# Attention means on chip, one load for the values, and the first weight loads among the keys and queries

## The chip, the cores and the metric

One core of one Trainium2 chip runs one program. The metric is the device time of that program in microseconds. The engines named below are PE (matrix products), DVE (VectorE), ACT (ScalarE), POOL (GpSimd) and SP, which here only issues DMAs.

## The reference

Inputs are q, k and v of 4 batches, 8 heads, 768 tokens and 64 features, and the parameters of a gated two-layer network. Every block of 32 tokens has a summary: the maximum of its keys and the mean of its values. Each query attends to the tokens less than 16 away and to the 24 summaries. The result goes through the network, token by token.

```python
k_sum = k.reshape(B, H, nb, block, D).max(axis=3)
v_sum = v.reshape(B, H, nb, block, D).mean(axis=3)
scores_l = np.where(|i - j| < 16, scale * q @ k.T, -1e9)
scores_s = scale * q @ k_sum.T + log(block)
a = softmax(concat(scores_l, scores_s))
x = a @ concat(v, v_sum)                  # (4, 768, 512) after joining heads
xk, xr = mix(mu_k, x, x_prev), mix(mu_r, x, x_prev)
out = sigmoid(xr @ w_r) * (relu(xk @ w_k)**2 @ w_v)
```

The network's weights come in 64-bit words, which the kernel turns into floats on chip.

## The kernel before, in words

**Attention.** Heads are taken in pairs: four pairs a batch, each a *set* with two *units* (the halves of the tokens, six windows of 64 queries each). A window sees 120 rows: 64 tokens, 24 summaries, 32 tokens. `load_set` (L302) loads the keys `kt` and, per half, the values `vx`: rows 0 to 63 by one DMA (L312), rows 88 to 119 by another (L315). DVE reduces the keys (L325 to L337). The mean of the values goes into rows 64 to 87. In batch 0 that is done from `vx` itself: POOL clears rows 64 to 87 (L346), PE multiplies each of the 12 windows by a shifted 120 x 24 pooling matrix and adds all 12 up in one PSUM tile (L350), ACT copies the sum out (`vm`, L367), and one DMA per half spreads it over the six windows (L370). The other batches take the means from a load of transposed values (L361 to L365) and spread them by the same DMAs. `unit` (L375) is then: scores on PE (L396), mask and row minimum on DVE (L407), exponential on ACT (L411), reciprocal on DVE (L417, L418), normalisation on POOL (six instructions a unit, L423), transposes on PE (L430), their copy on ACT (L434), products with the values on PE (L443), copy to `vx` (L454 on DVE or L456 on ACT).

**Network.** Work goes in eight half batches n. `mixes` makes the shifted blends, split in a high and a low part (L466 to L477); `gate_tile` is 12 matmuls of 512 columns against `wr` (L489 to L491) and a sigmoid (L495); `experts` goes over eight slices j, with 12 matmuls against `wk` (L510), relu, square and split (L515 to L521), 9 matmuls against `wv` (L531). The gates of n = 1 are put between the slices j = 1, 2, 3 of n = 0.

**Weights.** `weight` (L252) handles one of 20 pieces (4 `wr`, 8 `wk`, 8 `wv`) of 512 KB: a load into one of three `st` buffers (L260); a scaling on ACT (L268) or POOL (L271); three bit operations on DVE (L275, L278, L282); a cast on ACT (L290); a difference on DVE (L292).

**Order.** Nothing is issued in the order written. Each operation has a length from the table `LENGTH`, sometimes a second engine it may run on, and a due time. `Plan.schedule` (L111) hands due times back from users to producers (less the length and `SLACK`) and then simulates the five engines; at each step it places the operation that can start first, the most urgent where several can, and where there are two engines takes the one that would finish first. A load may be placed no sooner than 15 us (`EARLY`) before it is due, and its simulated rate is `DMA_NS_PER_BYTE`. The order of each engine that comes out is fixed: a real engine waits for its next instruction even if a later one is ready. The `wr` pieces have no due time of their own (L579), only that handed back from the gates.

```python
start, need, ok = max(at, now, o.due - EARLY if e == "SP" else 0), {}, True
...
if any(max(start, engines[f]) + c < start + o.ways[e][0] for f, (c, _) in o.ways.items() if f != e):
    continue
```

Of the kernel before, what the change touches and what calls it, by code (L numbers as in the profile page):

```python
# [29 lines left out]
HW = NW // 2  # L30
# [8 lines left out]
LENGTH = dict(  # L39
    score=900, transpose=340, vtrans=200, vpool=2800, values=1000, gate=2790, gate32=3720, e1=2090, e1_32=2800,  # L40
    e2a=1400, e2b=700, e2=700, e2_32=2800, e2l_32=930,
    kred=860, kred2=470, kmax=190, kcopy=340, vred=860, mask=204, rc=310, evac=475, mixd=535, sub=475, khv=300,
    result=695, wbits=340, wor=612, wsub=612, tiny=60,
    exp=380, pts=380, vm=160, mixa=520, cast=405, relu=525, square=435, sigmoid=500, wscale=570, wcast=530,
    norm=455, wscale_p=900, mixa_p=750, kcopy_p=600, evac_a=480, fill=900,
)
TAIL = dict(PE=0, DVE=85, ACT=95, POOL=0, SP=0)
LATENCY = dict(PE=260, DVE=110, ACT=110, POOL=150, SP=0)
DMA_NS_PER_BYTE = 1 / 290.0
DMA_FIXED = 2000  # L50
# [23 lines left out]
class Plan:  # L74
# [36 lines left out]
    def schedule(self):  # L111
# [83 lines left out]
@with_exitstack  # L195
def tile_kernel(ctx: ExitStack, tc: tile.TileContext, q, k, vT, v, mask, ident, pool, mu, w_k, w_v, w_r, out):
    nc = tc.nc
# [3 lines left out]
    def tiles(name, n, shape, dtype=F32, pool=const):  # L201
        return [pool.tile(shape, dtype, name=f"{name}{i}") for i in range(n)]
# [48 lines left out]

    def weight(name, i, src, dst_h, dst_l):  # L252
        st, we, wc = buf("st"), buf("we"), buf("wc")
# [31 lines left out]
        op("SP", "load", None, load, writes=[(st, 0)], size=P * 4096)  # L285
        op("ACT", "wscale", None, scale_act, reads=[(st, 0)], writes=whole, other=("POOL", "wscale_p", scale_pool))
# [12 lines left out]
    def windows(vw):  # L299
        return vw.t[0:NK, 0:S].rearrange("p (w d) -> p w d", d=P)  # L300

    def load_set(b, p):  # L302
# [39 lines left out]
        if b == 0:  # L342
            tp = buf("mm")

            for x in vw:
                op("POOL", "fill", None, lambda x=x: nc.gpsimd.memset(x.t[QW:KB, 0:S], 0.0), writes=[(x, "b")])  # L346
# [7 lines left out]
            op("PE", "vpool", None, means, reads=[(x, y) for x in vw for y in "abc"] + [*POOLM], writes=[(tp, 0)])  # L354
# [12 lines left out]
        op("ACT", "vm", None, lambda: nc.scalar.activation(  # L367
            vm.t, tp.t[0:NS, 0:P], AF.Copy, scale=1.0 / BLOCK if b else 1.0), reads=[(tp, 0)], writes=[(vm, 0)])
        for x in vw:
            op("SP", "load", None, lambda x=x: nc.sync.dma_start(  # L370
                out=windows(x)[QW:KB], in_=vm.t.unsqueeze(1).broadcast_to([NS, HW, P])),
               reads=[(vm, 0)], writes=[(x, "b")], size=NS * HW * 512)
        return e

    def unit(b, p, hf, e, due):  # L375
# [62 lines left out]
        def values():  # L438
# [252 lines left out]
```

## Time and profile before

| | |
|---|---|
| runs | 480.15 us median of 3 (479.31 to 1084.43) |
| the profiled execution's own time | 480.32 us |
| its span, first to last instruction | 478.5 us |
| mean granted PE clock | 0.966 |
| PE busy | 450.2 us (94%) |
| DVE, ACT, POOL busy | 275.4, 290.9, 125.4 us |

The profile covers one execution. A busy time is that of an engine over a stretch; idle time ahead of an instruction is put down to what ended it. L-numbers are lines of the kernel before.

### The profile page before, as it was taken

Reading aid. Unit: us, or ns where it says so; the run is one execution under the profiler, and the core shown is the slowest. Engines: PE = TensorE matmul, PEld = TensorE weight load, DVE = VectorE, ACT = ScalarE, POOL = GpSimd, SP = SyncE. Lnnn points to the kernel's source line nnn. Section 1 sums busy time; section 2 is a strip of 40 time slices with the busy share of each in tenths; the row PEclk is TensorE's granted clock in tenths of the full one; section 3 lists DMA queues with packets and bytes.
Section 4 is the critical chain, followed back from the end, with each engine's and each line's share of the span. In section 5 each row is a group of like instructions: output and inputs, shape, how many; then the busy total and the mean of one; then the engine's idle time right before and its main releaser. Section 6 shows DMA issues by size and latency. Waiting matters only on the chain.

```text
span 478.5 us, 9637 instructions
## 1 busy us (share of the span) xinstructions
PE 450.2 (94%) x3468; PEld 378.4 (79%) x3468; DVE 275.4 (58%) x876; ACT 290.9 (61%) x810; POOL 125.4 (26%) x258
## 2 busy tenths in 40 slices
PE   4878797889999999999999999999999999999996
PEld 3656585769888888888788888997788888888995
DVE  2669997779955486527454566429355564222223
ACT  3659789796778656527895565528886555231321
POOL 5527903205135402301433302202242302000000
PEclk9987589799999999999999999999999999999999
DMA  8896328775510119605200309806100010001001
GB/s 262 193 270 176 115 85 270 215 236 172 172 53 14 42 44 301 165 0 184 77 14 14 110 2 284 189 0 209 28 10 8 14 47 20 0 1 66 1 0 66
DMA packets 27893, 49.38 MB, mean 103 GB/s; under 512 B 3399, under 2 KB 16455, under 8 KB 27847
## 3 DMA queue, kind: packets, MB, share of 16 engines
q1 hardware_dynamic: 27847, 48.79, 35.2%
q8 instruction: 27, 0.44, 0.4%
q14 instruction: 19, 0.16, 0.1%
HBM read 40.12 MB, written 6.29 MB: 97 GB/s over the span
## 4 chain that ended last, share of the span: by engine, by line
PE 77%; ACT 6%; DVE 2%; issue 1%; POOL 1%; POOLq 0%; ACTq 0%
PE mm L531 27%; PE mm L510 26%; PE mm L489 4%; PE av L443 4%; PE mm L490 4%; PE mm L491 4%; PE pt L430 4%; PE sc L396 3%; ACT y L411 2%; ACT L411 1%; POOL y L423 1%; ACT L495 1%; ACT wc L268 1%; DVE wc L282 0%; ACT wv_h L290 0%
## 5 line engine op out<-in xcount | busy, mean ns | idle before, releaser
L423 POOL TENSOR_SCALAR y<-y,rc 128x120 f32<-128x120 f32 x192 | 87.2, 472 | 173.2 <-DVE rc L418 154.7
L510 PE MATMUL mm<-xs,wk_h 128*128 128x384 f32 x512 | 101.1, 339 | 2.0 <-ACT r L515 1.1
L510 PEld LDWEIGHTS mm<-xs,wk_h 128*128 128x128 f32 x512 | 90.2, 188 | 7.5 <-ACT z L495 1.4
L515 ACT ACTIVATE r<-mm 128x384 f32<-128x384 f32 x64 | 31.2, 487 | 96.3 <-PE mm L510 96.2
L411 ACT ACTIVATE y<-y,mn 128x120 f32<-128x120 f32 x192 | 73.7, 386 | 13.4 <-DVE mn L407 13.2
L531 PE MATMUL mm<-wv_h,kh 128*128 128x512 f32 x192 | 78.6, 409 | 2.0 <-ACT z L495 2.0
L531 PE MATMUL mm<-wv_l,kh 128*128 128x512 f32 x192 | 75.7, 394 | 0.0
L531 PE MATMUL mm<-wv_h,kl 128*128 128x512 f32 x192 | 60.0, 407 | 0.0
L407 DVE CUSTOM_DVE_ANT_0 y<-sc,mask_sb 128x120 f32<-128x120 f32 x192 | 43.6, 276 | 25.2 <-PE sc L396 16.7
L519 DVE CAST kh<-r 128x384 fp32r<-128x384 f32 x39 | 14.9, 382 | 73.6 <-ACT r L517 73.3
L510 PE MATMUL mm<-xs,wk_l 128*128 128x384 f32 x256 | 55.2, 337 | 0.0
L477 DVE TENSOR_TENSOR xs<-xa,xs 128x384 fp32r<-128x384 f32 x64 | 34.8, 553 | 22.2 <-ACT xs L475 22.0
L510 PEld LDWEIGHTS mm<-xs,wk_l 128*128 128x128 f32 x256 | 45.6, 188 | 0.0
L531 PEld LDWEIGHTS mm<-wv_h,kh 128*128 128x128 f32 x192 | 36.1, 188 | 9.6 <-ACT z L495 2.4
L489 PE MATMUL mm<-wr_h,xs 128*128 128x512 f32 x96 | 40.5, 422 | 2.7 <-ACT r L515 2.7
L472 DVE SCALAR_TENSOR_TENSOR xa<-vx,mu_sb,xa 128x384 f32<-128x384 f32 x64 | 40.4, 653 | 4.5 <-POOL xa L469 4.1
L430 PE MATMUL pt<-ident_sb,y 128*120 128x128 f32 x192 | 36.3, 298 | 7.0 <-ACT pts L434 5.8
L434 ACT COPY pts<-pt 120x384 f32<-120x384 f32 x64 | 30.2, 472 | 20.2 <-PE pt L430 20.2
L531 PEld LDWEIGHTS mm<-wv_l,kh 128*128 128x128 f32 x192 | 36.2, 188 | 5.8
L521 DVE TENSOR_TENSOR kl<-r,kh 128x384 fp32r<-128x384 f32 x64 | 36.7, 574 | 6.9 <-ACT kh L520 4.1
L531 PEld LDWEIGHTS mm<-wv_h,kl 128*128 128x128 f32 x192 | 34.6, 190 | 7.7 <-issue 0.6
L490 PE MATMUL mm<-wr_l,xs 128*128 128x512 f32 x96 | 39.2, 409 | 0.0
(54 smaller groups left out, 655.8 us busy)
## 6 DMA issues: line engine op xcount, KB each, us to landing
kt<-in_k SPq DMA_DIRECT2D x15, 544.0 KB
qt<-in_q SPq DMA_DIRECT2D x32, 192.0 KB
vx<-in_v SPq DMA_DIRECT2D x32, 192.0 KB
out<-z SPq DMA_DIRECT2D x24, 256.0 KB
st<-in_vT SPq DMA_DIRECT2D x12, 384.0 KB
st<-in_w_k SPq DMA_DIRECT2D x8, 512.0 KB
st<-in_w_v SPq DMA_DIRECT2D x8, 512.0 KB
vx<-in_v SPq DMA_DIRECT2D x32, 96.0 KB
```

The costliest lines, as they stand in the source:

```text
L407: op("DVE", "mask", None, lambda h=h, i=i, var=var: nc.vector.tensor_tensor_reduce(out=y[h].t[:, i, :], in0=sc[h].t[:, i, 0:NK], in1=mask_ ...
L411: op("ACT", "exp", None, lambda h=h, i=i: nc.scalar.activation(y[h].t[:, i, :], y[h].t[:, i, :], AF.Exp, bias=mn[h].t[:, i:i + 1], scale=-1.0,
L423: op("POOL", "norm", None, lambda h=h, i=i: nc.gpsimd.tensor_scalar(out=y[h].t[:, i, :], in0=y[h].t[:, i, :], scalar1=rc.t[:, NSL * h + i: ...
L430: nc.tensor.transpose(out=pt[h].t[0:NK, i * P:(i + 1) * P], in_=y[h].t[:, i, :], identity=ident_sb)
L472: op("DVE", "mixd", None, lambda xt=xt, xa=xa, p=p: nc.vector.scalar_tensor_tensor(out=xa.t, in0=xt.t[:, 1 + lo:1 + lo + HT], scalar=mu_sb ...
L477: op("DVE", "sub", None, lambda xa=xa, xh=xh, xl=xl: nc.vector.tensor_tensor(out=xl.t, in0=xa.t, in1=xh.t.bitcast(F32), op=ALU.subtract), ...
L489: nc.tensor.matmul(ps.t, xh.t[:, ts], wr_h[:, p, :], start=(p == 0), stop=False)
L490: nc.tensor.matmul(ps.t, xh.t[:, ts], wr_l[:, p, :], start=False, stop=False)
L510: nc.tensor.matmul(ps.t[:, 0:HT], w[:, j, p, :], x[p][s].t, start=(n == 0), stop=(n == 11))
L515: op("ACT", "relu", None, lambda: nc.scalar.activation(r.t, ps.t[:, 0:HT], AF.Relu), reads=[(ps, 0)], writes=[(r, 0)])
L521: op("DVE", "sub", None, lambda: nc.vector.tensor_tensor(out=kl.t, in0=r.t, in1=kh.t.bitcast(F32), op=ALU.subtract), reads=[(r, 0), (kh, 0 ...
L531: nc.tensor.matmul(acc[t].t, a.t[:, t * P:(t + 1) * P], w[:, j, :], start=start, stop=stop)
```

## The change

- `v` is laid out in memory with 24 zero rows at 64 to 87, so that each half is one DMA of 120 partitions (the two DMAs and POOL's clearing go). This holds for all batches.
- In batch 0 the 12 pooling matmuls go to four column groups of PE, three windows to each: the pooling matrix is 32 columns wide, and the sums stand in four groups of 32 partitions. ACT copies all 128, one matmul with a 128 x 24 selection matrix `sel` gathers 24 rows at partitions 64 to 87, ACT copies these, and POOL or DVE copies them into the six windows of each half. The eight DMAs of batch 0 that did this go; the other batches keep theirs.
- The loads of the four `wr` pieces are due at 0, 6, 12 and 18 us.
- The cast of a weight piece may also run on POOL.
- The planner's numbers: several lengths, a load rate of 340 instead of 290 bytes a ns, `SLACK` 400 instead of 300, PE's lengths times 1.6 before 25 us.

```diff
-    ... vpool=2800 ... square=435 ... norm=455, wscale_p=900, mixa_p=750, kcopy_p=600, evac_a=480
+    ... vpool=900, vsel=240, spread=560, spread_p=900 ... square=530 ...
+    norm=345, wscale_p=640, wcast_p=640, mixa_p=860, kcopy_p=630, evac_a=375
-DMA_NS_PER_BYTE = 1 / 290.0
+DMA_NS_PER_BYTE = 1 / 340.0
-SLACK = 300
+SLACK = 400
+COLD = 25000
+WR = 0, 6000
...
+            if e == "PE" and start < COLD:
+                o.cost *= 1.6
...
         op("ACT", "wcast", None, lambda: nc.scalar.copy(out=dst_h, in_=wc.t.bitcast(F32)),
-           reads=whole, writes=[((name, i), "h")])
+           reads=whole, writes=[((name, i), "h")],
+           other=("POOL", "wcast_p", lambda: nc.gpsimd.tensor_scalar(
+               out=dst_h, in0=wc.t.bitcast(F32), scalar1=1.0, scalar2=1.0, op0=ALU.mult, op1=ALU.mult)))
...
-                out=windows(vw[hf])[0:QW], in_=v[b, p, 0:QW, hf * HW:(hf + 1) * HW]),
-               writes=[(vw[hf], "a")], size=QW * HW * 512)
-            op("SP", "load", None, lambda hf=hf: nc.sync.dma_start(
-                out=windows(vw[hf])[KB:NK], in_=v[b, p, QW:LK, hf * HW:(hf + 1) * HW]),
-               writes=[(vw[hf], "c")], size=32 * HW * 512)
+                out=windows(vw[hf]), in_=v[b, p, :, hf * HW:(hf + 1) * HW]),
+               writes=[(vw[hf], "a"), (vw[hf], "b")], size=NK * HW * 512)
...
-                for w in range(NW):
-                    nc.tensor.matmul(
-                        tp.t[0:NS, 0:P], pool_sb[:, NS - 2 - 2 * w:2 * NS - 2 - 2 * w], windows(vw[w // HW])[:, w % HW, :],
-                        start=(w == 0), stop=(w == NW - 1))
+                for i in range(3):
+                    for g in range(4):
+                        w = 3 * g + i
+                        nc.tensor.matmul(
+                            tp.t[32 * g:32 * g + 32, 0:P], pool_sb[:, 4 - 2 * i:36 - 2 * i],
+                            windows(vw[w // HW])[:, w % HW, :], start=(i == 0), stop=(i == 2))
...
+        if b == 0:
+            sp, t2 = buf("sp"), buf("mm")
+            op("ACT", "vm", None, lambda: nc.scalar.copy(out=sp.t, in_=tp.t[:, 0:P]), ...)
+            op("PE", "vsel", None, lambda: nc.tensor.matmul(
+                t2.t[QW:KB, 0:P], sel_sb, sp.t, start=True, stop=True), ...)
+            op("ACT", "vm", None, lambda: nc.scalar.copy(out=vm.t[QW:KB], in_=t2.t[QW:KB, 0:P]), ...)
+            for x in vw:
+                def spread(eng, x=x):
+                    return lambda: eng.tensor_copy(
+                        out=windows(x)[QW:KB], in_=vm.t[QW:KB].unsqueeze(1).broadcast_to([NS, HW, P]))
+                op("POOL", "spread_p", None, spread(nc.gpsimd), reads=[(vm, 0)], writes=[(x, "b")],
+                   other=("DVE", "spread", spread(nc.vector)))
...
-        weight("wr", i, w_r[i * P:(i + 1) * P, :], *places("wr", i))
+        weight("wr", i, w_r[i * P:(i + 1) * P, :], *places("wr", i), due=WR[0] + WR[1] * i)
```

## Rows read from the trace of the kernel before

**Rows 1.** By stretch: length, busy us of PE, PEld, DVE, ACT, POOL, granted clock, DMA.

```profile
0.00:10.00 10.00, 3.42 (x34) 2.63 (x35) 3.08 (x17) 2.58 (x8) 6.27 (x16) 1.00 0.84 241
10.00:34.60 24.60, 19.97 (x250) 15.60 (x248) 13.74 (x63) 14.40 (x57) 8.34 (x24) 0.97 0.89 244
34.60:61.50 26.90, 21.50 (x247) 15.48 (x246) 25.60 (x90) 22.40 (x78) 21.64 (x31) 0.63 0.55 165
61.50:107.20 45.70, 38.99 (x221) 31.20 (x219) 37.32 (x92) 39.22 (x77) 8.70 (x14) 0.90 0.62 194
107.20:478.50 371.30, 366.35 (x2721) 313.51 (x2721) 195.61 (x617) 212.29 (x594) 80.47 (x173) 1.00 0.26 75
```

**Rows 2.** PE's waits from 61.5 us on: who for whom, us, times, longest.

```profile
PE mm L489 <- ACT r L515: 2.7, 1, 2.7
PE mm L531 <- ACT z L495: 2.0, 1, 2.0
PE mm L510 <- ACT r L515: 1.1, 1, 1.1
PE mm L510 <- ACT z L495: 0.9, 1, 0.9
```

**Rows 3.** DVE's timeline before 31 us: start, us, instruction, idle before it and its end.

```profile
8.37 0.28 DVE L407 CUSTOM_DVE_ANT_0 y<-sc,mask_sb 128x120 f32<-128x120 f32 x1 [2.83 <-DMA mask_sb<-in_mask]
...
22.42 0.28 DVE L407 CUSTOM_DVE_ANT_0 y<-sc,mask_sb 128x120 f32<-128x120 f32 x1 [1.68 <-PE sc L396]
...
27.60 0.95 DVE L325 TENSOR_REDUCE kg<-kt 128x48 f32<-128x768 f32 x1 [1.96 <-DMA kt<-in_k]
...
30.23 0.43 DVE L275 TENSOR_SCALAR we<-st 128x512 uint32<-128x512 uint32 x1 [1.04 <-DMA st<-in_w_r]
```

**Rows 4.** SP's timeline: three of the four loads of `wr`.

```profile
23.91 1.37 SPq L260 DMA_DIRECT2D st<-in_w_r  x3
```

**Rows 5.** Groups of the first 61.5 us: count, busy us, mean ns, idle before.

```profile
L350 PE MATMUL mm<-vx,pool_sb 120*24 120x128 f32 x96 | 13.3, 305 | 2.0 <-DMA vx<-in_v 1.1 <-DMA pool_sb<-in_pool 1.0
L443 PE MATMUL av<-pts,vx 120*64 120x64 f32 x192 | 12.4, 274 | 2.3 <-ACT pts L434 1.8 <-DMA vx<-vm 0.5
L292 DVE TENSOR_TENSOR wr_l<-wc,wr_h 128x512 fp32r<-128x512 f32 x4 | 2.7, 682 | 0.0
L367 ACT ACTIVATE vm<-mm 24x128 f32<-24x128 f32 x4 | 1.1, 265 | 3.0 <-PE mm L350 3.0
```

**Rows 6.** PE's timeline, 12 to 32 us: scores of a unit, pooling of a set.

```profile
12.92 0.85 PE L396 MATMUL sc<-kt,qt 64*64 64x120 f32 x24
...
27.04 2.80 PE L350 MATMUL mm<-vx,pool_sb 120*24 120x128 f32 x24
```

**Rows 7.** POOL's timeline: normalisations of two units, a scaling, three blends.

```profile
20.91 2.06 POOL L423 TENSOR_SCALAR y<-y,rc 128x120 f32<-128x120 f32 x6 [0.59 <-DVE rc L418]
...
34.86 0.65 POOL L271 TENSOR_SCALAR wc<-st 128x512 f32<-128x512 f32 x1 [6.99 <-DVE wr_l L292]
...
54.44 4.54 POOL L423 TENSOR_SCALAR y<-y,rc 128x120 f32<-128x120 f32 x6 [0.42 <-ACT pts L434]
...
72.03 3.90 POOL L469 TENSOR_SCALAR xa<-vx,om_sb 128x384 f32<-128x384 f32 x3
```

**Rows 8.** DVE's timeline: one operation ahead of POOL's blends and beside them.

```profile
70.52 0.69 DVE L282 SCALAR_TENSOR_TENSOR wc<-wc,we 128x512 uint32<-128x512 uint32 x1
...
74.11 0.99 DVE L282 SCALAR_TENSOR_TENSOR wc<-wc,we 128x512 uint32<-128x512 uint32 x1
```

**Rows 9.** ACT's groups, 61.5 to 107.2 us: count, busy us, mean ns.

```profile
L268 ACT ACTIVATE wc<-st 128x512 f32<-128x512 f32 x9 | 6.0, 671 | 1.4 <-DVE wv_l L292 1.0 <-DVE wk_l L292 0.4
L290 ACT CAST wv_h<-wc 128x512 fp32r<-128x512 f32 x6 | 3.7, 615 | 0.5 <-DVE wc L282 0.5
L290 ACT CAST wk_h<-wc 128x512 fp32r<-128x512 f32 x4 | 2.5, 619 | 0.0
L495 ACT ACT_TABLE_LOAD x4 | 5.1, 1283 | 0.1
```

**Rows 10.** The chain that ended last: gate matmuls near 67 us and near 90 us.

```profile
67.67 0.23 PE mm L489
...
90.11 0.43 PE mm L490
```

More of the change, by code (lines that the diff above doesn't have):

```diff
@@ L39 @@
 LENGTH = dict(
-    score=900, transpose=340, vtrans=200, vpool=2800, values=1000, gate=2790, gate32=3720, e1=2090, e1_32=2800,
+    score=900, transpose=340, vtrans=200, vpool=900, vsel=240, spread=560, spread_p=900, values=1000, gate=2790, gate32=3720, e1=2090, e1_32=2800,
     e2a=1400, e2b=700, e2=700, e2_32=2800, e2l_32=930,
@@ L43 @@
     result=695, wbits=340, wor=612, wsub=612, tiny=60,
-    exp=380, pts=380, vm=160, mixa=520, cast=405, relu=525, square=435, sigmoid=500, wscale=570, wcast=530,
-    norm=455, wscale_p=900, mixa_p=750, kcopy_p=600, evac_a=480, fill=900,
+    exp=380, pts=380, vm=160, mixa=520, cast=405, relu=525, square=530, sigmoid=500, wscale=570, wcast=530,
+    norm=345, wscale_p=640, wcast_p=640, mixa_p=860, kcopy_p=630, evac_a=375, fill=735,
 )
@@ L195, in tile_kernel @@
 @with_exitstack
-def tile_kernel(ctx: ExitStack, tc: tile.TileContext, q, k, vT, v, mask, ident, pool, mu, w_k, w_v, w_r, out):
+def tile_kernel(ctx: ExitStack, tc: tile.TileContext, q, k, vT, v, mask, ident, pool, sel, mu, w_k, w_v, w_r, out):
     nc = tc.nc
@@ L206, in tile_kernel @@
         kg=tiles("kg", 2, [P, 49]), ks=tiles("ks", 2, [P, NS]),
-        vs=tiles("vs", 1, [P, NS]), vm=tiles("vm", 4, [NS, P]),
+        vs=tiles("vs", 1, [P, NS]), vm=tiles("vm", 4, [P, P]), sp=tiles("sp", 2, [P, P]),
         y=tiles("y", 4, [P, NSL, NK]), mn=tiles("mn", 4, [P, NSL]), sm=tiles("sm", 3, [P, 2 * NSL]),
@@ L230, in tile_kernel @@
     wr_l = const.tile([P, NCK, DM], F32R, name="wr_l")
-    pool_sb = const.tile([NK, 2 * NS - 2], F32, name="pool_sb")
-    MASK, IDENT, MU, OM, POOLM = [((x, 0),) for x in ("mask", "ident", "mu", "om", "pool")]
+    pool_sb = const.tile([NK, 36], F32, name="pool_sb")
+    sel_sb = const.tile([P, NS], F32, name="sel_sb")
+    MASK, IDENT, MU, OM, POOLM, SEL = [((x, 0),) for x in ("mask", "ident", "mu", "om", "pool", "sel")]
     op("SP", "load", None, lambda: nc.sync.dma_start(out=mask_sb, in_=mask), writes=MASK, size=P * 3 * NK * 4)
@@ L236, in tile_kernel @@
     op("SP", "load", None, lambda: nc.sync.dma_start(out=pool_sb, in_=pool), writes=POOLM, size=22000)
+    op("SP", "load", None, lambda: nc.sync.dma_start(out=sel_sb, in_=sel), writes=SEL, size=12000)
     op("SP", "load", None, lambda: nc.sync.dma_start(out=ident_sb, in_=ident), writes=IDENT, size=65536)
@@ L249, in e2_due, with weight @@
         return e1_due(b, hf, j + 1) + 2200
-    def weight(name, i, src, dst_h, dst_l):
+    def weight(name, i, src, dst_h, dst_l, due=None):
         st, we, wc = buf("st"), buf("we"), buf("wc")
@@ L283, in join @@
                 out=wc.t, in0=wc.t, scalar=3, in1=we.t, op0=ALU.logical_shift_left, op1=ALU.bitwise_or)
-        op("SP", "load", None, load, writes=[(st, 0)], size=P * 4096)
+        op("SP", "load", due, load, writes=[(st, 0)], size=P * 4096)
         op("ACT", "wscale", None, scale_act, reads=[(st, 0)], writes=whole, other=("POOL", "wscale_p", scale_pool))
@@ L343, in load_set @@
             tp = buf("mm")
-            for x in vw:
-                op("POOL", "fill", None, lambda x=x: nc.gpsimd.memset(x.t[QW:KB, 0:S], 0.0), writes=[(x, "b")])
             def means():
-                for w in range(NW):
-                    nc.tensor.matmul(
-                        tp.t[0:NS, 0:P], pool_sb[:, NS - 2 - 2 * w:2 * NS - 2 - 2 * w], windows(vw[w // HW])[:, w % HW, :],
-                        start=(w == 0), stop=(w == NW - 1))
-            op("PE", "vpool", None, means, reads=[(x, y) for x in vw for y in "abc"] + [*POOLM], writes=[(tp, 0)])
+                for i in range(3):
[4 more added lines that the diff above has]
+                            windows(vw[w // HW])[:, w % HW, :], start=(i == 0), stop=(i == 2))
+            op("PE", "vpool", None, means, reads=[(x, y) for x in vw for y in "ab"] + [*POOLM], writes=[(tp, 0)])
         else:
@@ L366, in load_set @@
                 out=tp.t[0:NS, 0:P], in_=vs.t, identity=ident_sb), reads=[(vs, 0), *IDENT], writes=[(tp, 0)])
[L367 to L372, printed above, removed]
+        if b == 0:
+            sp, t2 = buf("sp"), buf("mm")
+            op("ACT", "vm", None, lambda: nc.scalar.copy(out=sp.t, in_=tp.t[:, 0:P]), reads=[(tp, 0)], writes=[(sp, 0)])
+            op("PE", "vsel", None, lambda: nc.tensor.matmul(
+                t2.t[QW:KB, 0:P], sel_sb, sp.t, start=True, stop=True), reads=[(sp, 0), *SEL], writes=[(t2, 0)])
+            op("ACT", "vm", None, lambda: nc.scalar.copy(out=vm.t[QW:KB], in_=t2.t[QW:KB, 0:P]),
+               reads=[(t2, 0)], writes=[(vm, 0)])
+            for x in vw:
[4 more added lines that the diff above has]
+                   other=("DVE", "spread", spread(nc.vector)))
+        else:
+            op("ACT", "vm", None, lambda: nc.scalar.activation(
+                vm.t[0:NS], tp.t[0:NS, 0:P], AF.Copy, scale=1.0 / BLOCK), reads=[(tp, 0)], writes=[(vm, 0)])
+            for x in vw:
+                op("SP", "load", None, lambda x=x: nc.sync.dma_start(
+                    out=windows(x)[QW:KB], in_=vm.t[0:NS].unsqueeze(1).broadcast_to([NS, HW, P])),
+                   reads=[(vm, 0)], writes=[(x, "b")], size=NS * HW * 512)
         return e
@@ L446, in values @@
                     )
-        op("PE", "values", due - 1000, values, reads=[(vw, x) for x in "abc"] + [(pts[0], 0), (pts[1], 0)],
+        op("PE", "values", due - 1000, values, reads=[(vw, x) for x in "ab"] + [(pts[0], 0), (pts[1], 0)],
            writes=[(av, 0)])
@@ L648 @@
     vn = np.stack([vn[:, :, w * QW:w * QW + LK] for w in range(NW)], axis=3)
+    vn = np.concatenate([vn[:, :, 0:QW], np.zeros_like(vn[:, :, 0:NS]), vn[:, :, QW:LK]], axis=2)
     i = np.arange(QW)[:, None]
@@ L661 @@
     mu = np.stack([np.asarray(inputs["moe_mu_k"]), np.asarray(inputs["moe_mu_r"])])
-    means = np.zeros((NK, 2 * NS - 2), np.float32)
-    means[WINDOW:WINDOW + BLOCK, NS - 2] = 1.0 / BLOCK
-    means[WINDOW + BLOCK:QW, NS - 1] = 1.0 / BLOCK
-    means[KB:KB + WINDOW, NS - 1] = 1.0 / BLOCK
+    means = np.zeros((NK, 36), np.float32)
+    means[WINDOW:WINDOW + BLOCK, 4] = 1.0 / BLOCK
+    means[WINDOW + BLOCK:QW, 5] = 1.0 / BLOCK
+    means[KB:KB + WINDOW, 5] = 1.0 / BLOCK
+    sel = np.zeros((P, NS), np.float32)
+    for n in range(NS):
+        sel[32 * (n // 6) + n % 6, n] = 1.0
     arrays = {
@@ L674 @@
         "pool": means,
+        "sel": sel,
         "mu": mu.reshape(2, NPAIR, P).transpose(2, 0, 1),
```

## The prediction

> **What bounds the kernel now.** I read first the busy times by stretch, then PE's waits, then the timelines of DVE, SP and POOL in the stretches that these pointed to.
>
> The stretches [rows 1] cut the span at two events: the first gate matmul at 61.5 us and the end of PE's last long wait at 107.2 us. Behind 107.2 PE is busy 366.35 of 371.3 us at the full clock: the kernel is bound by PE there, and nothing in this change takes matmuls of that part away. So the question is only how early PE gets into that state. Ahead of 61.5 us the engine to watch is DVE. Its busy time is 3.08 of 10 us, 13.74 of 24.6, and then 25.60 of 26.9: nearly idle first, then full. It stood idle for 6.92 + 10.86 + 1.30 = 19.1 us ahead of the first gate. Its waits [rows 3] say for what: the mask's DMA (2.83 us), scores that stood behind pooling matmuls on PE (1.68), keys of the fourth set (1.96), the first weight piece (1.04). The `wr` loads are not issued before 23.91 us [rows 4], so their bit work falls in the part where DVE is full. From 61.5 to 107.2 us PE has four long waits, all for ACT, together 2.7 + 2.0 + 1.1 + 0.9 = 6.7 us [rows 2]; ACT is busy 39.22 of 45.7 us there, DVE 37.32, POOL only 8.70 [rows 1]. After the longest wait 12 gate matmuls run at 0.43 us a piece, others at 0.23 [rows 10], so the wait costs a second time through the clock, which is granted at half (1.2 instead of 2.4 GHz) after PE stood still.
>
> **Part one: ahead of the first gate.** This is a budget of DVE's idle time.
>
> *The order of the loads.* By due times, the mask comes before the values of the first set, and `wr` pieces go between the first set's values, the second and third sets' keys and values. The bytes ahead of the gate are the same: 590 KB of zero rows are read, and 590 KB of spread means are no longer moved. The mask is then there when the scores are, which ends DVE's 2.83 us wait [rows 3] some 1.4 us sooner. A `wr` piece costs DVE 0.43 + 0.69 + 0.69 + 0.68 = 2.5 us [rows 3, 8, 5]. By 34.6 us the old kernel had done 4.3 us of this work (seven of the sixteen instructions); with three pieces landed by then it does 7.5, that is 3.2 more in idle time. Two more units' masks, about 3.3 us with their reciprocals, come before 34.6 too, since the 30.23 us stall for weights [rows 3] no longer has them queued behind it. So 1.4 + 3.2 + 3.3 = 7.9 of the 19.1 us are filled. Bounds: if DMA, busy 0.89 from 10 to 34.6 us [rows 1], only trades late weights for late values, 2; if all idle time behind the first 10 us goes, 12.
>
> *The means.* Pooling took PE 2.80 us a set [rows 6], 13.3 us in all [rows 5]. The nearest row for matmuls in several groups at once is a unit's scores, 12 matmuls on four quadrants in 0.85 us [rows 6]; if the column groups don't overlap it stays 2.8. I take 0.9, plus 0.25 for the selection. The new chain is pooling, copy, selection, copy (0.27 each, [rows 5]) and spreading, 2.5 to 3 us without a DMA, against 2.8 + 0.27 + two issues on SP and a landing. PE waited for that landing only 0.5 us in all [rows 5]; I count -0.5. The 8 us that PE gains here lie under DVE's idle time and are counted with it: the 1.68 us wait for scores is one of those filled. Pooling at the old price would give 1 to 2 us of it back. The selection is a new wait in PE's order: scores and transposes of other units stand behind it for about 0.3 us of ACT's copy, four times, and ACT's second copy waits in the same way with exponentials behind it; up to 1 us each, hidden while DVE has work.
>
> *Spreading and casts on POOL.* Spreading has no row. POOL's scaling of 512 elements takes 0.65 us and a normalisation of 120 takes 0.34 [rows 7]; the line through both gives 0.85 for the 768 elements of a half, and beside a busy DVE it is near double, as six normalisations take 2.06 us alone and 4.54 us there [rows 7]. So eight of them cost POOL 5 to 13 us; I take 8. Clearing, which goes, lay in POOL's idle first 8 us and is worth nothing. POOL was busy 21.64 of 26.9 us before the gate but 8.34 of 24.6 before that [rows 1], and three of the four spreads can fall there. What reaches DVE is the neighbourhood: the same bit operation takes 0.69 us ahead of POOL's blends and 0.99 beside them [rows 8]. With eight spreads and some three casts, half of them meeting a DVE operation of that kind, that is 11 x 0.5 x 0.3 = 1.6, so +1.5 us (0 to 5).
>
> The Trainium skill, "SBUF — State Buffer" (section "SBUF: two separate sides"), says of this that VectorE and GpSimd take a shared pair of ports as an exclusive lock, for VectorE's operations with two inputs in SBUF too, and that the later one fully blocks. By the lock alone each meeting could cost DVE a whole POOL instruction, 0.65 us or more: 11 x 0.5 x 0.65 = 3.6 us instead of 1.5. The trace shows the smaller loss for DVE and the larger one for POOL, so I stay with the rows.
>
> Part one: -7.9 - 0.5 + 1.5 = -6.9, so the first gate near 54.5 us.
>
> **Part two: 61.5 to 107.2 us, now moved forward.** The work to do is the same but for the cast, which may go to POOL. ACT had 9 scalings of 0.671 us and 10 casts of 0.617 [rows 9]. Scaling on POOL was priced at 900 ns and is now at 640, near the measured 0.65 [rows 7], as is the cast. With POOL nearly idle I expect half of the 19 to leave ACT, 6 us of its 39.2. PE's four waits of 6.7 us should shrink by two thirds, -4.5, and the slow gates (12 x 0.2 = 2.4 us) by -1.5. The ten POOL instructions cost DVE 10 x 0.5 x 0.3 = 1.5 us. Table loads, 1.28 us each [rows 9], follow from the order of sigmoids and exponentials and are not known to the planner; they may come out fewer or more by two either way, 2.6 us. Sum -4.5; bounds -9 (no wait and no slow gate left) and +3 (two more table loads on PE's path).
>
> **Part three: behind 107.2 us.** The 24 value DMAs saved there and the zero rows read lie under PE, with DMA busy 0.26 [rows 1]. A new order can open or close small gaps, 371.3 - 366.35 = 4.95 us at most to be won, of which part is the end; I take 0, and 2 either way.
>
> **The sum** is made against the profiled execution: 480.32 us, of which 478.5 are the span. 480.32 - 6.9 - 4.5 = 468.9. The median of 480.15 is 0.2 us from it, so I leave it at 468.9 us.
>
> **The rivals.**
>
> *Order without gain (473 to 479 us).* DMA is the bound of the first 35 us, and 2 MB of `wr` between keys and values put off the last set's values by up to 8 us. For it: DMA share 0.84 and 0.89 ahead of 34.6 us [rows 1]. Against it: DVE was the full engine behind 34.6 us, not DMA. Then 2 of part one and 2 of part two are left: 476.
>
> *More than that (456 to 463).* The first gate goes to where the loads allow: all landed at about 37 us (9.1 MB at 244 GB/s [rows 1]), plus some 9 to 11 us of means, normalising, values, blends and split, 46 to 48 us, some -14, and part two loses most of its waits, -6: 460. For it: 11.2 us of DVE's idle time stay in my sum. Against it: DVE's own work, 42.4 us [rows 1], must fit in.
>
> *Slower: POOL as the bound.* The normalisations of a unit stand in POOL's fixed order behind a spread, and the spread behind a load that the planner, at 340 bytes a ns where the trace moved 241 to 244 GB/s [rows 1], thinks there some 10 us too early (the 9.1 MB ahead of the gate, by the sizes in the code, take 27 us at the one rate and 37 at the other). If POOL waits there at each of the last two sets and its 48 normalisations then run at 0.76 us as at 54.44 [rows 7], POOL's 36.25 us ahead of the gate, become 30.7 (5.6 of clearing, nearly all of the 6.27 us in the first ten, are gone) + 13 of spreads + 5 of casts + 20 of waiting: first gate at 68, +7, and DVE loses 4 more: 491. It decides when POOL has no idle time from 20 us to the gate. Against it: every late load delays the other engines alike, and POOL had over 16 us idle from 10 to 34.6.
>
> *The change doesn't do what it says:* the planner gives the cast to POOL hardly ever; then part two is worth -1 and the time is 472.5, within the first case's range.
>
> **How the numbers follow.** The forecast has 0.55 (463 to 473 us), order without gain 0.24, more than that 0.15, slower 0.06. A difference of 2%, about what a measurement of this kernel can tell from no change, is at 470.5. Two thirds of the forecast's case and all of the better one are below: 0.37 + 0.15 = 0.52. Slower by over 2% is most of the POOL case, 0.05, and 0.43 is left. The range 458 to 478 us leaves out the slow case, the top of the second and the bottom of the third.
>
> **What would show it.** Right: first gate matmul at 53 to 57 us; DVE busy over 18 us from 10 to 34.6; a pooling group of 0.9 us a set; casts on POOL, and PE's waits for ACT behind the gate under 3 us; PE's 371 us behind them unchanged. Wrong: first gate at 59 us or later with DVE idle again behind 34.6, waiting for loads; or POOL full ahead of it; or PE's waits for ACT as long as before.

## The result, and the profile after

| | before | after |
|---|---|---|
| median of 13 runs each | 480.05 us (478.50 to 481.54, and one of 1084.43) | 475.51 us (473.94 to 478.47) |
| ratio, with its 95% interval | | 0.9915 (0.9895 to 0.9936) |
| profiled execution, its span | 480.32, 478.5 us | 474.88, 473.1 us |
| first gate matmul | 61.5 us | 56.3 us |
| from there to the end | 417.0 us | 416.8 us |

The ratio leaves out the one run of 1084.43 us. The change gains 0.85%, 4.5 us, where 11.3 were forecast. In the two profiled executions the whole gain lies ahead of the first gate; behind it nothing was won. The busy times of the changed kernel by stretch, cut at its own gate, answer to [rows 1] (columns as there):

```profile
0.00:10.00 10.00, 3.55 (x48) 2.52 (x48) 3.97 (x19) 3.66 (x13) 0.40 (x8) 1.00 0.82 247
10.00:34.60 24.60, 18.80 (x272) 13.31 (x276) 19.60 (x82) 16.45 (x66) 15.25 (x29) 0.86 1.03 296
34.60:56.30 21.70, 17.03 (x220) 11.66 (x220) 20.65 (x71) 17.04 (x59) 19.34 (x31) 0.77 0.26 81
56.30:102.00 45.70, 40.00 (x202) 32.21 (x202) 40.88 (x88) 34.05 (x68) 12.00 (x18) 0.89 0.68 213
102.00:473.10 371.10, 366.04 (x2741) 313.04 (x2739) 194.20 (x626) 214.02 (x600) 74.64 (x170) 1.00 0.28 81
```

The third busy time of a row is DVE's: 19.60 of 24.6 us from 10 to 34.6, where it was 13.74. Ahead of the gate DVE is now idle for 12.1 us instead of 19.1. The fourth row is the disappointment. ACT is busy 34.05 of 45.7 us, 5.2 less than in the old kernel's stretch of equal length, and DVE 40.88, 3.6 more, and PE waits nearly as long as before, as its list of waits shows (answering to [rows 2]):

```profile
PE mm L529 <- ACT z L514: 4.0, 1, 4.0
...
PE mm L508 <- ACT r L534: 1.5, 1, 1.5
```

5.5 us in place of 6.7. What ACT itself waited for in that stretch is in its own list, changed kernel first, then the kernel before from 61.5 to 107.2 us:

```profile
ACT wk_h L296 <- DVE wc L288: 3.7, 4, 1.8
ACT wc L274 <- DVE wv_l L300: 3.3, 3, 1.7
ACT wc L274 <- DVE wk_l L300: 1.8, 2, 1.1
```

```profile
ACT wc L268 <- DVE wv_l L292: 1.0, 2, 0.8
...
ACT wv_h L290 <- DVE wc L282: 0.5, 1, 0.5
ACT wc L268 <- DVE wk_l L292: 0.4, 1, 0.4
```

ACT spent the time that it was relieved of in waits for weight pieces from DVE: these three groups and 0.7 us for the `wv` casts make 9.5 us, against 1.9 in the kernel before. The other way round DVE has less to wait for: 1.1 us for ACT's casts instead of 7.8. Of the two the fuller one behind the gate is now DVE (the lists again with the changed kernel first):

```profile
DVE wk_l L300 <- ACT wk_h L296: 1.1, 1, 1.1
```

```profile
DVE wv_l L292 <- ACT wv_h L290: 6.3, 3, 3.5
DVE wk_l L292 <- ACT wk_h L290: 1.5, 1, 1.5
```

The 4.0 us wait can be followed in ACT's timeline (start, us, instruction, idle before):

```profile
88.96 1.28 ACT L430 ACT_TABLE_LOAD   x1
90.26 0.40 ACT L430 ACTIVATE y<-y,mn 128x120 f32<-128x120 f32 x1
...
93.39 1.28 ACT L514 ACT_TABLE_LOAD   x1
94.69 0.60 ACT L514 ACTIVATE z<-mm 128x512 f32<-128x512 f32 x1
```

The gate tile's last matmul starts at 88.85 us, but its sigmoid runs at 94.69: ahead of it stand four exponentials of the next batch, a scaling, two casts and two table loads. PE's next e1 (the 12 products with `wk`) needs the PSUM tile that this sigmoid frees. The planner doesn't see the hurry: a sigmoid's due time comes back only from the last product of its half batch, which DVE makes some 80 us later (174.32 to 176.41 us).

### The profile page after: what moved, and what is told of

It is laid out like the page before. It is cut to its first block, busy times and chain, and to the rows that moved or that the text cites. A ratio compares the mean times of both kernels' runs of the same rounds, so it can differ in the third digit from the quotient of the medians.

```text
span 473.1 us, 9589 instructions
## 1 busy us (share of the span) xinstructions
PE 445.4 (94%) x3476; PEld 372.7 (79%) x3476; DVE 279.3 (59%) x882; ACT 285.2 (60%) x806; POOL 121.6 (26%) x256
## 4 chain that ended last, share of the span: by engine, by line
PE 74%; ACT 8%; DVE 7%; DMA 6%; issue 2%; POOL 2%; SPq 1%; ACTq 0%; DVEq 0%; POOLq 0%
PE mm L550 27%; PE mm L529 26%; PE av L462 4%; PE pt L449 4%; DMA st<-in_w_r 3%; PE mm L508 3%; PE mm L510 3%; PE mm L509 3%; PE sc L415 3%; ACT y L430 2%; DMA kt<-in_k 2%; POOL y L442 2%; ACT L430 1%; DVE we L284 1%; ACT pts L453 1%
## 5 line engine op out<-in xcount | busy, mean ns | idle before, releaser
L442 POOL TENSOR_SCALAR y<-y,rc 128x120 f32<-128x120 f32 x192 | 83.5, 454 | 153.7 <-DVE rc L437 127.7
L529 PE MATMUL mm<-xs,wk_h 128*128 128x384 f32 x512 | 102.4, 342 | 4.1 <-ACT z L514 4.0
L529 PEld LDWEIGHTS mm<-xs,wk_h 128*128 128x128 f32 x512 | 91.5, 190 | 10.2 <-ACT z L514 5.0
L534 ACT ACTIVATE r<-mm 128x384 f32<-128x384 f32 x64 | 31.3, 489 | 94.2 <-PE mm L529 94.1
L430 ACT ACTIVATE y<-y,mn 128x120 f32<-128x120 f32 x192 | 73.7, 386 | 11.9 <-DVE mn L426 11.4
L488 POOL TENSOR_SCALAR xa<-vx,om_sb 128x384 f32<-128x384 f32 x25 | 21.4, 863 | 87.5 <-DVE xs L496 83.3
L449 PE MATMUL pt<-ident_sb,y 128*120 128x128 f32 x192 | 37.3, 300 | 5.3 <-ACT pts L453 3.3
L508 PE MATMUL mm<-wr_h,xs 128*128 128x512 f32 x96 | 39.5, 412 | 1.5 <-ACT r L534 1.5
L462 PEld LDWEIGHTS av<-pts,vx 120*64 120x64 f32 x768 | 28.9, 147 | 13.6 <-issue 8.4
```

Source lines behind the costliest of these rows:

```text
L430: op("ACT", "exp", None, lambda h=h, i=i: nc.scalar.activation(y[h].t[:, i, :], y[h].t[:, i, :], AF.Exp, bias=mn[h].t[:, i:i + 1], scale=-1.0,
L442: op("POOL", "norm", None, lambda h=h, i=i: nc.gpsimd.tensor_scalar(out=y[h].t[:, i, :], in0=y[h].t[:, i, :], scalar1=rc.t[:, NSL * h + i: ...
L449: nc.tensor.transpose(out=pt[h].t[0:NK, i * P:(i + 1) * P], in_=y[h].t[:, i, :], identity=ident_sb)
L462: nc.tensor.matmul(av.t[hs, w * QW:(w + 1) * QW], windows(vw)[:, w, hs], pts[h].t[:, i, c * QW:(c + 1) * QW], start=True, stop=True,)
L508: nc.tensor.matmul(ps.t, xh.t[:, ts], wr_h[:, p, :], start=(p == 0), stop=False)
L529: nc.tensor.matmul(ps.t[:, 0:HT], w[:, j, p, :], x[p][s].t, start=(n == 0), stop=(n == 11))
```

## The experiments

Medians are of three rounds (4 to 10 runs); the ratio is to the kernel before, on the same chip. Times of single points (first gate) are from one profiled execution; six kernels with the same order ahead of the gate, or nearly, have it between 56.3 and 58.6 us, so a microsecond or two there says nothing. Nor is the first gate the time: the means alone have it 10.6 us sooner than the kernel before and gain 4.1, and the lengths alone don't have it later and are 0.6% slower.

| kernel | us | ratio (95%) | first gate |
|---|---|---|---|
| sixth sigmoid first | 473.37 | 0.9845 (0.9808 to 0.9882) | 56.8 |
| exponential for sigmoid (another function) | 470.12 | 0.9804 (0.9762 to 0.9846) | 57.4 |
| casts back on ACT | 474.79 | 0.9881 (0.9851 to 0.9911) | 56.7 |
| sigmoid with a due time | 476.50 | 0.9922 (0.9890 to 0.9953) | 58.2 |
| due times alone | 485.59 | 1.0114 (1.0081 to 1.0147) | 62.3 |
| means alone | 475.64 | 0.9910 (0.9873 to 0.9946) | 50.9 |
| means alone, sixth sigmoid first | 475.58 | 0.9916 (0.9889 to 0.9943) | 50.4 |
| means alone, pooling three times | 483.73 | 1.0080 (1.0046 to 1.0114) | 60.0 |
| planner's numbers alone | 491.58 | 1.0237 (1.0202 to 1.0273) | 68.1 |
| numbers but the load rate | 485.87 | 1.0149 (1.0104 to 1.0195) | 63.5 |
| lengths and slack alone | 482.01 | 1.0064 (1.0033 to 1.0095) | 59.5 |
| changed, without due times | 481.26 | 1.0033 (1.0005 to 1.0060) | 59.9 |
| means and due times | 473.61 | 0.9881 (0.9848 to 0.9915) | 57.9 |
| changed, tanh | 470.19 | 0.9796 (0.9766 to 0.9825) | 58.6 |
| before, tanh | 469.45 | 0.9791 (0.9750 to 0.9832) | 61.1 |
| means, due times, tanh | 469.59 | 0.9779 (0.9736 to 0.9821) | 57.3 |
| changed, tanh, third buffer | 469.29 | 0.9790 (0.9770 to 0.9811) | 57.3 |
| means, due times, tanh, third buffer | 468.25 | 0.9758 (0.9727 to 0.9789) | 58.2 |

**Which part gained.** The due times alone:

```diff
-        weight("wr", i, w_r[...], *places("wr", i))
+        weight("wr", i, w_r[...], *places("wr", i), due=WR[0] + WR[1] * i)
```

> Edit: the kernel before with nothing but the due times 0, 6, 12 and 18 us for the loads of the wr pieces. Theory A for the part ahead of the gate (DVE's idle time is filled by weight work): about 3 of the 5.2 us, first gate near 58.5 us, ratio 0.994. Rival M (the means on chip and PE's 8 us give the gain): first gate not earlier than 61 us, ratio 1.000 or above, since the values come later.

Measured 1.1% slower, gate at 62.3 us, as rival M has it. DVE's idle time ahead of the gate fell, though only from 19.1 to 16.5 us, and what filled it is not what the gate needs: DVE's bit operations ahead of the gate are those of nine pieces, where the same view of the kernel before has seven:

```profile
L279 DVE SCALAR_TENSOR_TENSOR we<-st,we 128x512 uint32<-128x512 uint32 x9 | 6.5, 718 | 0.1
```

The means alone (one load of the values, grouped pooling, selection, spread; old numbers, no due times, no cast on POOL), and the same with the pooling loop run three times in the same order:

```diff
-                for i in range(3):
+                for i in (0, 1, 2) * 3:
```

> Edit: the kernel before with the one load of the values and the means on chip alone (lengths only for the operations that are new; old rate, slack and lengths, no due times for wr, no cast on POOL). The due times alone were 1.1% slower, with weight work for two more pieces in DVE's former idle time and the first gate no earlier. Theory E: what moves the gate is that scores no longer stand behind 2.8 us of pooling on PE from 20 to 31 us; first gate near 58 us, ratio 0.993. Rival F: neither part does it alone, since DVE is full behind 34.6 us either way: gate at 61 us or later, ratio 0.998 to 1.005.

> Edit: the kernel with the means alone, its planned order kept, but the twelve grouped pooling matmuls of a set are issued three times over (the sums restart each time), so that PE pays 2.6 us or more a set again. Theory G: the gain of the means (first gate matmul at 50.9 instead of 61.5 us, first e1 at 61.3 instead of 71.0, ratio 0.991) is PE's time, since scores of the next units stand behind pooling on PE: then the first e1 comes 3 to 7 us later and the ratio goes to 0.998 or above. Rival H: the gain is that the spread no longer goes through SP and a DMA, and that ACT's and PE's orders differ: then the first e1 moves by less than 2 us, ratio 0.990 to 0.995.

The means alone give all of the gain, 0.9910: theory E, with the gate sooner than it expected. PE's timeline, first of the means alone, then with the loop three times:

```profile
21.25 0.86 PE L350 MATMUL mm<-vx,pool_sb 120*32 120x128 f32 x24
...
25.39 0.84 PE L411 MATMUL sc<-kt,qt 64*64 64x120 f32 x24
```

```profile
21.49 2.17 PE L350 MATMUL mm<-vx,pool_sb 120*32 120x128 f32 x72
...
28.34 0.42 PE L350 MATMUL mm<-vx,pool_sb 120*32 120x128 f32 x5 [2.11 <-issue]
...
30.31 1.48 PE L411 MATMUL sc<-kt,qt 64*64 64x120 f32 x24
```

Pooling a set takes 0.86 us where it took 2.80 [rows 6], and 2.17 with the loop three times. There the scores that stand behind two sets' pooling come 5 us later, and the gate and the first e1 9.1. DVE does the same work ahead of the gate in both (34.5 and 34.7 us) and is idle for 25.3 us instead of 16.5; its waits for scores are 6.4 us instead of 1.9. So time on PE, through the scores that stand behind it, is enough to lose the whole gain: theory G, and by more than it expected. It gives no price for a microsecond of pooling. Pooling costs 6.9 us more in all (11.4 against 4.5), 2.1 us are the pause of PE in the middle of the second set, for which the trace names no cause, and the mean clock granted ahead of the gate is 0.83 instead of 0.95. What the one load and the spread without a DMA are worth by themselves was not tried.

The planner's numbers, and their parts:

```diff
-DMA_NS_PER_BYTE = 1 / 290.0
+DMA_NS_PER_BYTE = 1 / 340.0
...
+            if e == "PE" and start < COLD:
+                o.cost *= 1.6
```

> Edit: the kernel before with the planner's numbers alone (lengths, load rate 340, slack 400, PE's lengths times 1.6 before 25 us). Theory E: no work and no transfer changes, so only the order of each engine does: within 2 us of the kernel before, ratio 0.996 to 1.004. Rival N (the better lengths make the order fit the chip, and the gain is theirs): first gate 3 us earlier, ratio 0.994 or below.

> Edit: the kernel with the planner's numbers alone (2.4% slower than before, DVE waiting 11.2 us for keys), but with the old load rate of 290 bytes a ns. Theory R: the rate of 340 is the culprit: the plan believes that keys are there too early and puts reductions at the head of DVE's order; with 290 DVE's waits for keys fall back to 5 us and the ratio to 0.998 to 1.006. Rival S: the lengths or PE's factor of 1.6 did it: ratio 1.018 or above.

> Edit: the kernel before with the new lengths and the slack of 400 alone (old load rate, no factor of 1.6 for PE). The numbers cost 2.4% together and 1.5% without the rate. Theory S: the lengths for POOL, which are those of an idle DVE, put too much on POOL ahead of the gate: ratio 1.010 or above. Rival Q: the factor of 1.6 for PE did the rest: ratio 0.997 to 1.005.

Neither theory on the numbers alone holds: by themselves they cost 2.4%. The two runs on their parts (1.0149 and 1.0064) also lie between what their two theories expected. DVE's waits in the kernel with all the numbers, from 8 to 58 us:

```profile
DVE kg L328 <- DMA kt<-in_k: 11.2, 3, 7.1
```

DVE waited 4.8 us for keys before; with the old rate the same view has 0.5. By differences of medians the lengths with the slack cost 0.6%, PE's factor 0.9%, the rate 0.9%. A mechanism, the waits for keys, is shown for the rate alone.

> Edit: the changed kernel without the due times for the wr loads. Theory E: the due times add little to the means: first gate within 1.5 us of 56.3, ratio 0.990 to 0.994. Rival F (the early loads pay only where the pooling is gone from PE's path): first gate 3 us later, ratio 0.997 or above.

> Edit: the kernel with the means alone plus the due times 0, 6, 12 and 18 us for the wr loads, under the old planner numbers. Theory G: DVE has 5.1 us idle from 34.6 us back to 10 in the means alone kernel less, and its gates wait for wr_l and xs (0.9 and 2.0 us), so earlier wr pieces help: 1 to 4 us better than the means alone, ratio 0.983 to 0.989. Rival K: as in the kernel with the due times alone, the idle time fills with pieces for the experts and nothing moves or it gets slower, ratio 0.991 to 1.002.

Without the due times the gate is 3.6 us later and the gain is gone: rival F. They are worth 1.2% inside the change, where they make up for what the numbers cost; on the means alone they are worth 0.3% (in theory G's range, but inside the intervals).

**Why the second part gave nothing.**

```diff
+    sig = [o for o in order if o.name == "sigmoid"][5]
+    order.remove(sig)
+    order.insert(next(i for i, o in enumerate(order) if o.name == "exp" and o.n > sig.n), sig)
```

> Edit: the changed kernel, its planned order kept, but the sixth sigmoid (third gate tile of n = 1) is moved ahead of the first exponential of batch 1 on ACT. Theory A (order on ACT): PE's 4.0 us wait at 91.3 us is for this sigmoid, which stands behind four exponentials, two table loads and the masks that these wait for; with it go the wait and the half-speed stretch behind it (e1 4.2 instead of 2.1 us, scores 1.4 instead of 0.8): 6.7 us, time near 469, ratio to the kernel before 0.977. Rival D (DVE, busy 40.9 of 45.7 us behind the first gate, is the bound): PE waits elsewhere instead, at most 1.5 us gained, ratio 0.987 to 0.991.

The wait is gone, 4.0 us and the slow matmuls behind it, but by the medians only 2.1 us remain won, between the two theories. Behind 90 us others stand in its place (PE's timeline):

```profile
96.21 0.83 PE L415 MATMUL sc<-kt,qt 64*64 64x120 f32 x20 [1.89 <-DVE mn L426]
...
107.15 1.67 PE L529 MATMUL mm<-xs,wk_h 128*128 128x384 f32 x8 [1.24 <-ACT r L534]
```

The same move on the means alone gave nothing (0.9916 against 0.9910, rival D):

> Edit: the kernel with the means alone, order kept, with the sixth sigmoid moved ahead of the first exponential of batch 1, as was done with the changed kernel (2.1 us there). Theory A: PE's 2.6 us wait for this sigmoid goes, with a part coming back as waits for masks: 1 to 3 us better than the means alone, ratio 0.985 to 0.989. Rival D: no change, 0.991.

A due time for the sigmoids, which makes the whole plan anew, gave nothing either (rival D):

> Edit: the changed kernel, in which a sigmoid gets a due time of its own, 3 us behind its gate tile's, so that the planner itself places it ahead of the exponentials that are ready with it. Theory A (order on ACT): PE's 4.0 us wait for the sixth sigmoid shrinks, but one exponential and a pair of table loads stay ahead of it: 1 to 3 us better than the changed kernel, ratio 0.984 to 0.990. Rival D: no change, ratio 0.9915.

The casts back on ACT (`o.emit = o.ways["ACT"][1]` for those that the plan gave to POOL):

> Edit: the changed kernel, its planned order kept, but every weight cast that the plan gave to POOL is issued on ACT at the same place. Theory A: ACT's load is not what PE waits for behind the first gate, so within 1.5 us of the changed kernel, ratio 0.988 to 0.994, with the first gate no later (POOL, busy 19.3 of the last 21.7 us ahead of it, has less to do). Rival C (as I had predicted: the casts on POOL relieve an ACT that bounds): 2 us or more slower than the changed kernel, ratio 0.995 or above.

No slower, as theory A has it: the cast on POOL is worth nothing. Then the table loads, which ACT makes when it goes from exponentials to sigmoids and back: first with the exponential in the sigmoid's place, which leaves the gate's function out, then with one that gives the same gate, sigmoid(x) = (1 + tanh(x/2)) / 2:

```diff
-nc.scalar.activation(z[t].t, ps.t, AF.Sigmoid)
+nc.scalar.activation(z[t].t, ps.t, AF.Tanh, scale=0.5)
...
-nc.scalar.activation(r.t, r.t, AF.Square)
+nc.scalar.activation(r.t, r.t, AF.Square, scale=0.5**0.5)
...
-nc.vector.tensor_tensor(out=z[t].t, in0=acc[t].t, in1=z[t].t, op=ALU.mult)
+nc.vector.scalar_tensor_tensor(
+    out=z[t].t, in0=z[t].t, scalar=1.0, in1=acc[t].t, op0=ALU.add, op1=ALU.mult)
```

> Edit: the changed kernel, order kept, with the exponential function in place of the sigmoid in the gates, so that the table loads of 1.28 us go and nothing else moves (the gate's function is left out). Theory A: the two table loads behind the third tile of n = 1 are 2.6 of its 5.6 us delay; PE's wait falls from 4.0 to about 1.4 us and the slow stretch is shorter: 3 to 5 us gained, ratio 0.980 to 0.985. Rival D: less than 1 us, ratio 0.988 to 0.991.

> Edit: the changed kernel, order kept, with the gate computed as half of one plus the hyperbolic tangent of half the argument: the half goes into the square's scale, the one into the last product, and no instruction is added. Theory T (the waits of part two are the table loads between exponentials and sigmoids): all loads but the first go, with the right function, so as with the exponential in its place, ratio 0.978 to 0.984. Rival D (DVE bounds part two): within 1 us of the changed kernel, ratio 0.990.

> Edit: the same hyperbolic tangent in the kernel before, order kept. Theory T: of its 6.7 us of PE waits for ACT behind the first gate, with eight table loads among them, the greater part goes, and the slow gates with it: 5 to 8 us better than before, ratio 0.983 to 0.990. Rival D: less than 2 us, ratio 0.996 or above.

The trace of the changed kernel with tanh has one load of a table in all, the first:

```profile
L430 ACT ACT_TABLE_LOAD x1 | 1.3, 1283 | 0.7 <-PEq L706 0.7
```

This agrees with the Trainium skill, "ScalarE: Activation LUTs" (section "Table sets: the hidden batching unit"): tables come in sets, and tanh is in that of exp as well as in that of sigmoid. It counts about 2.7 us for a load. Here a load takes 1.283 us, and in ACT's timeline above the next instruction starts 0.02 us behind it (88.96 + 1.28, 90.26).

The exponential (0.9804) and tanh (0.9796) come out alike, as theories A and T have it. The kernel before gains 2.1%, 10.1 us where 5 to 8 were expected, and the changed kernel 1.2 points. Without table loads the change is worth nothing that the intervals show: 0.9796 and 0.9791. Of the old kernel's waits behind its gate at 61.1 us these are left:

```profile
PE mm L489 <- ACT r L515: 0.5, 1, 0.5
PE mm L510 <- ACT z L495: 0.4, 1, 0.4
PE sc L396 <- DVE mn L407: 0.2, 1, 0.2
```

The changed kernel with tanh keeps 4.0 us of such waits behind its gate at 58.6 us:

```profile
PE mm L529 <- ACT z L514: 1.9, 1, 1.9
PE mm L508 <- ACT r L534: 1.5, 1, 1.5
PE mm L529 <- ACT r L534: 0.6, 1, 0.6
```

ACT in turn waits 13.0 us for DVE there, from 60 to 110 us:

```profile
ACT wk_h L296 <- DVE wc L288: 4.6, 6, 1.8
ACT wc L274 <- DVE wv_l L300: 3.1, 2, 1.7
ACT wc L274 <- DVE wk_l L300: 2.9, 3, 1.1
ACT wv_h L296 <- DVE wc L288: 2.4, 3, 1.2
```

A third buffer for the scaled weights takes the second and third of these away (`x.t = three[x.n % 3]` for each scaled weight, after planning):

> Edit: the changed kernel with the hyperbolic tangent, order kept, with three buffers for the scaled weights instead of two, handed out in turn after the planning. Open: PE still waits 4.0 us for ACT behind the gate there, while ACT waits 13 us for DVE's weight work, 6.0 of it for a free buffer (scalings) and 7.0 for joined words (casts). Theory W: a scaling that waits for its buffer at the head of ACT's order delays the relu or sigmoid that PE needs; without it PE's waits fall to 2 us or less: 2 to 3 us better than with two buffers, ratio 0.973 to 0.976. Rival D (DVE itself, 44.7 of 45.7 us busy there, holds all of it, so the wait moves to the cast): less than 1 us, ratio 0.978 to 0.981.

> Edit: the kernel with the means and the due times under the old numbers, with the hyperbolic tangent. If both theories hold, the gains add: 0.988 less about 0.010, so 0.975 to 0.982. If the waits only change places, 0.985 or above.

> Edit: the same third buffer in the kernel with the means, the due times, the old numbers and the hyperbolic tangent, where ACT waits 4.2 us for a free buffer and PE 2 to 3 us for ACT. Theory W: 1 to 2 us better than with two, ratio 0.973 to 0.976. Rival D: 0.977 to 0.980.

In the changed kernel the waits for a buffer go and those for the joined words grow (the same view):

```profile
ACT wk_h L296 <- DVE wc L288: 6.4, 4, 3.7
ACT wv_h L296 <- DVE wd L288: 4.1, 3, 2.2
...
ACT wk_h L296 <- DVE wd L288: 1.8, 1, 1.8
```

7.0 has become 12.3 us, and the time stays (0.9790 against 0.9796): rival D, for the changed kernel. With the means, the due times and the old numbers the third buffer comes out where theory W had it (0.9758 against 0.9779), but within the intervals, so that it stays open there. Two rows, of the kernel before and the changed one, both with tanh, each for 45.7 us from its gate, show what fills these stretches (columns as in [rows 1]):

```profile
61.10:106.80 45.70, 44.69 (x262) 37.08 (x262) 45.02 (x107) 35.08 (x83) 17.65 (x20) 0.98 0.75 231
58.60:104.30 45.70, 42.04 (x231) 34.53 (x231) 45.42 (x97) 31.54 (x70) 15.41 (x18) 0.98 0.76 234
```

DVE is full in both, and PE nearly so in the kernel before. DVE ends the last weight piece at 113.6 us (before, tanh: 112.90 + 0.68), 114.8 (changed, tanh) and 113.5 (with the third buffer), wherever the gate is; with the table loads it was 122.3 (before) and 116.0 (changed). Up to there DVE is busy for 94.2 us in the kernel before with tanh and 99.0 in the changed one, of which the spreads are some 4. So an earlier gate finds DVE with no idle time left to fill. That DVE's work holds the time there is argued from these numbers; no run took work from DVE.

The means with the due times and tanh (0.9779) lie in the range of gains that add, since I had counted 0.010 for tanh. By what tanh gave the kernel before, 2.1%, a sum would be 0.967, so the gains don't add in full. That kernel with a third buffer is the fastest, 468.25 us, 1.5% below the changed one; its interval overlaps those of the other tanh kernels.

## Why the prediction was right or wrong

**Part one** was -6.9 and came to -5.2 us. The budget holds as a sum: DVE's idle time ahead of the gate fell by 7.0 (forecast 7.9) and its work rose by 1.8 (1.5). Its terms were laid at the wrong door. I gave 7.9 us to the order of the loads and 0.5 to the means, with the sentence that PE's 8 us "lie under DVE's idle time and are counted with it". By the medians the means alone gave 4.1 us and the loads alone lost 5.3: they made DVE busy with pieces for the experts. The runs with the means alone say why: with pooling longer on PE, DVE does the same work and is idle 8.9 us more. An engine's idle time is no gain until one knows which of its ready work goes there. How much of the old kernel's idle time is due to this is not shown: only 2.7 of the 19.1 us are put down to scores there, 8.4 to keys and 2.8 to the mask. So it is luck that the signs for this part came true (gate at 56.3 us, DVE busy 19.60 us from 10 to 34.6).

That the work rose by 1.8 is luck too. The +1.5 us stood for POOL's neighbourhood; the rise is 4.0 us of spreads, which I had put on POOL, less about 2.6 of bit operations that now come behind the gate. The price of one meeting was right: of three blends just ahead of the gate the two beside POOL took 0.94 and 1.02 us, and the third, when POOL had ended (54.58 + 0.96), took 0.60. That is 0.34 and 0.42 more, near the 0.3 that I took and not the whole POOL instruction of 0.65:

```profile
54.07 0.94 DVE L491 SCALAR_TENSOR_TENSOR xa<-vx,mu_sb,xa 128x384 f32<-128x384 f32 x1
54.93 1.02 DVE L491 SCALAR_TENSOR_TENSOR xa<-vx,mu_sb,xa 128x384 f32<-128x384 f32 x1
55.88 0.60 DVE L491 SCALAR_TENSOR_TENSOR xa<-vx,mu_sb,xa 128x384 f32<-128x384 f32 x1
```

```profile
53.55 1.05 POOL L488 TENSOR_SCALAR xa<-vx,om_sb 128x384 f32<-128x384 f32 x1
54.58 0.96 POOL L277 TENSOR_SCALAR wc<-st 128x512 f32<-128x512 f32 x1
```

The spread was costed on the wrong engine: the planner gave seven of eight to DVE, at 0.598 us each:

```profile
L380 DVE COPY vx<-vm 24x768 f32<-24x768 f32 x7 | 4.0, 598 | 0.1
```

**Part two** is where the prediction failed, -4.5 against -0.2. The step was that casts on POOL relieve ACT and so shrink PE's waits by two thirds; they went from 6.7 to 5.5 us. ACT was relieved by 5.2 us, but mainly by table loads (four instead of eight, 5.1 us) and by four exponentials that fall outside the stretch, and hardly by casts (five of 21 scalings and casts ran on POOL, not half); with the casts back on ACT the time was no worse. ACT's busy time was not what PE waited for: ACT's order, the table loads and the weight work on DVE in front of it were. Moving one sigmoid gave 2.1 us, taking out the table loads 5.3; what PE still waits for ACT then goes with ACT's own waits for DVE. I had named the loads as 2.6 us either way; taking them all out gives 10 us in the old kernel.

**The planner's numbers** had no term at all in my sum, and no reason was given for that. They issue nothing, and still cost 2.4% alone, since they set every engine's order; as far as these runs tell, the due times served mainly to win that back. The slow rival's premise, loads believed there too early, was sound, but it strikes at the keys on DVE and not at POOL. (That rival's sum was also short: it has the 48 normalisations at 0.76 us, which is 36.5 us, but adds them up with the 23.5 that they took in the old kernel.)

The time came out in the range of the rival without gain, and not for its reason: DVE's waits for keys ahead of the gate fell from 8.4 to 5.6 us, and the first gate did move. POOL had idle time throughout (2.4 of the last 21.7 us ahead of the gate), so the slow rival fell. Part three held: PE is busy for all but 5.1 of the last 371.1 us.

## What to carry to other kernels

Test an idle engine's worth by what its fixed order would put there, and see whether the work is on the way to the next event that matters. Two functions of ACT that alternate are worth a look before any other engine is relieved: where one can be written in terms of a function in the other's set, the table loads go, here without one instruction more. When a planner's numbers change, price the order they make, and measure the edit and the numbers apart.

## What the runs showed that I had not expected

A wait of the same length can cost differently through PE's clock. These are two executions, one of each kernel. In the changed kernel, after 3.99 us of waiting, the next 12 e1 matmuls and 24 scores take 5.55 us (95.33 to 100.88 us, PE's timeline):

```profile
95.33 2.93 PE L529 MATMUL mm<-xs,wk_h 128*128 128x384 f32 x8 [3.99 <-ACT z L514]
98.06 1.48 PE L529 MATMUL mm<-xs,wk_l 128*128 128x384 f32 x4
99.47 1.48 PE L415 MATMUL sc<-kt,qt 64*64 64x120 f32 x24
100.88 1.65 PE L529 MATMUL mm<-xs,wk_h 128*128 128x384 f32 x8
```

With the casts back on ACT, after 3.96 us, the same work takes 4.59 us (94.97 to 99.56):

```profile
94.97 2.34 PE L529 MATMUL mm<-xs,wk_h 128*128 128x384 f32 x8 [3.96 <-ACT z L514]
97.11 1.48 PE L529 MATMUL mm<-xs,wk_l 128*128 128x384 f32 x4
98.52 1.11 PE L415 MATMUL sc<-kt,qt 64*64 64x120 f32 x24
99.56 1.66 PE L529 MATMUL mm<-xs,wk_h 128*128 128x384 f32 x8
```

The busy times by stretch have the clock granted from 95 to 99.5 us at 0.50 (1.2 of 2.4 GHz) in the one and 0.62 in the other, and from 99.5 to 102 us at 0.72 and 1.00. That is 0.96 us between two waits of equal length, a fifth of what the whole change gained. Why the clock came back sooner in the one is not shown.
